# A feed-forward layer's third K tile: 64 channels padded with zeros to 128 rows

## The chip, the cores and the metric

The kernel runs on one core of a Trainium2 chip, as a single launch. The metric is the device time of the execution in microseconds (us), from the first to the last instruction; lower is better. All arithmetic is float32.

## What is computed

Two blocks follow each other. The first is a recurrence over 768 tokens, for 4 batches and 8 heads with 40 channels each; the second is a feed-forward layer on its 3072 output rows of 320 channels:

```
state = zeros(B, H, D, D)                       # B, H, S, D = 4, 8, 768, 40
for t in range(S):
    y[t]  = r[t] @ state
    Sa    = state @ a[t]
    state = state * w[t] - outer(Sa, b[t]) + outer(v[t], k[t])
x = y as (B*S, H*D)                             # 3072 x 320
h = x @ w_in                                    # 320 x 2048
out = (h - tanh(h)) @ w_out                     # 2048 x 320
```

## The kernel before

The recurrence goes in 24 chunks of 32 tokens, all batches and heads at once. `prep(c)` does what needs no state: transposes of the inputs (`p_nat`), products over tokens (`p_prod`), and the inverse of a triangular matrix, built in four doublings. Each doubling is a chain that passes from engine to engine: four transposes on TensorE (`p_flip`, line 246), a copy on ScalarE (`t`, line 247), four products (`p_g`), a masked multiplication on VectorE (`g`, line 280), four products (`p_z`), a subtraction on VectorE (`z`, line 285). `chain(c)` does what needs the state (`p_u`, `p_s`, `p_st`, `p_y`) and ends in `turn`, which transposes 128 tokens of the output by `p_x` and copies them into a half of `x_t` (in the profile `xT`), 128 rows of channels by 3 K tiles by 256 tokens. Its 320 channels are K tiles of 128, 128 and 64 (`KT`), so in the third tile rows 0 to 63 are written and read, by line 384.

After every second chunk the layer for 256 tokens is put on a list (`todo`), and `tick()` issues one piece of it at a time among the chains of the following chunks, so that TensorE has work while the chains wait. A piece is a pair of `w_in` blocks of 128 columns: into one PSUM bank `p_h` go, for each of the two blocks, three products over the K tiles (`mm` of line 85, with `w1` as the loaded weights and `x_t` streamed, 256 columns). The float32 product is two matmuls on the chip, each with a weight load of its own, so a pair of blocks is 12 matmuls. Then come ScalarE (tanh, and two squares, lines 397 to 399), GpSimd (403, 404) and VectorE (402, 405, 406, 408, 409), which leave h - tanh(h) in `gt`. Eight such pieces are followed by two products with `w2` (`p_o`, 16 blocks of 320 columns each, twice 32 matmuls), a copy (416) and a store. `p_h` and `p_o` share three PSUM banks (pool `psf`). The layer of the last 256 tokens has no chunk beside it and stands alone at the end; it will be called the last layer.

Once, at the start, the weights are loaded (`weights`), and constants are set on GpSimd. The scheduler of the language fixes each engine's order at build time; every engine then works in that order, and waits where its inputs are not there.

Each run of the two matmuls of a third K tile will be called a **visit**: there are 16 in a layer, 192 in the 12 layers, of which 176 stand among the chunks and 16 in the last layer.

Of the kernel before, what the change touches and what calls it, by code (L numbers as in the profile page):

```python
"""RWKV-7 state recurrence followed by a tanh-shrink feed-forward layer, on one core.

The recurrence runs over chunks of 32 tokens, all batches and heads at a time.  Inside a
chunk, with P the running product of the decays, it is a unit lower triangular system

    (I + N) U = -(A V + Â S0),   A[t,s] = â_t.k̂_s,  N[t,s] = â_t.b̂_s  (s < t)
    â_t = P[t-1] a_t,  k̂_s = k_s / P[s],  b̂_s = b_s / P[s]

whose inverse is built exactly, by doubling the inverted diagonal blocks from 1 to 32.
Then  Y = P[t-1] (R S0 + tril(R V^T) K̂ + tril(R U^T) B̂)  and  # L10
      S = P[31] (S0 + V^T K̂ + U^T B̂).
A tile of 128 partitions holds the 32 tokens of each of the four batches; the matrices
over tokens are block diagonal.  Heads go in pairs of 2 x 64 partitions (40 used) where
channels are on the partitions; states are kept per pair as block diagonal matrices.

All that holds for decays whose products over a chunk, and their quotients, fit float32.
The kernel looks at them, and at whether all outputs are finite; if need be it ends with
the recurrence token by token and the layer on its result.
"""
# [11 lines left out]
F32 = mybir.dt.float32  # L31
# [7 lines left out]
L = 32      # tokens in a chunk  # L39
DP = 64     # partitions that a head's channels take  # L40
P = 128
PR_MIN, PR_MAX = 1e-18, 1e12    # the products of a chunk's decays that the chunks' form is for

# h - tanh(h) = h s (C0 + s (C1 + C2 s + C3 s^2)), s = h^2 < SMALL^2, to 3e-9 of itself
SMALL = 0.25
C0, C1, C2, C3 = 0.33333333232863477, -0.13333281848327064, 0.05392688810132763, -0.02079906881679924
# C1 + C2 s + C3 s^2 = GAM - (SQ s + SQB)^2
SQ = math.sqrt(-C3)
# [5 lines left out]
def rwkv_shrink(ctx: ExitStack, tc: tile.TileContext, r, k, v, w, a, b, tok, dec, chan, w_in, w_out, out):  # L54
# [40 lines left out]
    # before[s, t] = 1 where s < t in one batch  # L95
# [4 lines left out]
    # pair_t[s, t] = -1 where s and t = s + 1 are a block of two  # L100
# [5 lines left out]
    # join[h][t, s] = 1 where t is in the second and s in the first half of one block of 2 h  # L106
    join = {}
# [9 lines left out]
    # own[p, b] = 1 where partition p is a token of batch b  # L117
# [4 lines left out]
    # half[p, e] = 1 where partition p is a channel of the pair's head e  # L122
# [4 lines left out]
    # what the scan of the decays adds: 1 before each batch's first token  # L127
# [5 lines left out]
    # of each chunk: the greatest and the least product of decays; 0, or NaN if an output isn't finite  # L133
# [6 lines left out]
    # the state, transposed: [(e, channel of k), batch, pair, e', channel of v], zero but for e = e'  # L140
# [7 lines left out]
    w1 = fixed("w1", [P, len(KT), DFF])  # L148
    w2 = fixed("w2", [P, NF, DM])
    WP = max(256, DM)  # L150

    def weight(dst, src, n):
        """A piece of a weight, [rows, n], into SBUF as float32."""
        rows = dst.shape[0]
        if src.dtype == F32:
            nc.sync.dma_start(out=dst, in_=src)
            return
        # float64 bits: sign 1, exponent 11, fraction 52, low word first (and values in float32's range).
        raw = ff.tile([P, WP, 2], I32, name="raw", tag="raw", bufs=1)[:rows, :n]
        nc.sync.dma_start(out=raw, in_=src.bitcast(I32).rearrange("p (n two) -> p n two", two=2))  # L160
        lo, hi = raw[:, :, 0], raw[:, :, 1]
        t_ = ff.tile([P, WP], I32, name="wt", tag="wt", bufs=1)[:rows, :n]
        f_ = ff.tile([P, WP], I32, name="wf", tag="wf", bufs=1)[:rows, :n]
        V.tensor_scalar(f_, hi, 0x07FFFFFF, 3, Alu.bitwise_and, Alu.logical_shift_left)
        V.tensor_scalar(t_, hi, -0x40000000, None, Alu.bitwise_and)
        V.tensor_tensor(f_, f_, t_, Alu.bitwise_or)
        V.tensor_scalar(t_, lo, 29, None, Alu.logical_shift_right)
        V.tensor_tensor(f_, f_, t_, Alu.bitwise_or)
        # to nearest: the first bit that is left out, added to the last one kept
        V.tensor_scalar(t_, lo, 3, 31, Alu.logical_shift_left, Alu.logical_shift_right)  # L170
        V.tensor_tensor(f_, f_, t_, Alu.add)
        # 0 below float32's normal numbers: the high words, as float32, rise with the magnitude
        V.tensor_scalar(t_, hi, 0x7FFFFFFF, None, Alu.bitwise_and)
        V.scalar_tensor_tensor(dst, t_.bitcast(F32), LEAST, f_.bitcast(F32), Alu.is_ge, Alu.mult)  # L174
# [12 lines left out]
    def tick():  # L187
        """The next piece of the layer, among the recurrence's chains."""
        while todo and next(todo[0], todo) is todo:
            todo.pop(0)  # L190

# [1 line left out]
    def prep(c):  # L193
# [10 lines left out]
        # the decays' running products: pr[..., i] is that of i tokens  # L204
# [3 lines left out]
        # (held to where quotients of them are sound: if one of them was not there, seen tells)  # L208
# [10 lines left out]
        # the state's decay over the chunk, for both halves of a pair  # L219
# [3 lines left out]
        # tokens on the partitions  # L223
# [45 lines left out]
        # z = ((I + N)^-1)^T by blocks of 2, 4, .. 32  # L269
# [20 lines left out]
        # -(I + N)^-1 A V and -((I + N)^-1 Â)^T  # L290
# [14 lines left out]
    def chain(c, g, x_t):  # L305
# [13 lines left out]
        if c > 0:  # L319
            # the old state's part of the output  # L320
            s_ = sb.tile([P, B, HP, 2, D], F32, name="s_", tag="s_")
            for b in range(B):
                p_ = bank("p_s")
                for q in range(HP):
                    T.transpose(p_[:, q * P:(q + 1) * P], st[:, b, q].rearrange("p e d -> p (e d)"), ident)  # L325
                A.copy(s_[:, b], p_.rearrange("p (q e d) -> p q e d", q=HP, e=2)[:, :, :, :D])
# [48 lines left out]
    def turn(yf, x_t, i_):  # L375
        """128 tokens of the layer's input, with the channels on the partitions."""
        p_ = bank("p_x")
        o_ = i_ * P
        for i, (r0, n) in enumerate(KT):
            T.transpose(p_[:n, i * P:(i + 1) * P], yf[:, r0:r0 + n], ident)  # L380
        full = sum(n == P for _, n in KT)
        A.copy(x_t[:, :full, o_:o_ + P], p_[:, :full * P].rearrange("p (k t) -> p k t", t=P))
        for i in range(full, len(KT)):
            A.copy(x_t[:KT[i][1], i, o_:o_ + P], p_[:KT[i][1], i * P:(i + 1) * P])

# [1 line left out]
    def layer(x_t, rows):  # L387
        gt = ff.tile([P, NF, 2 * P], F32, name="gt", tag="gt", bufs=1)
        for f in range(0, NF, 2):
            p_ = psf.tile([P, 512], F32, name="p_h", tag="pf")  # L390
            for i in range(2):
                for k_, (_, n) in enumerate(KT):
                    mm(p_[:, i * 2 * P:(i + 1) * 2 * P], w1[:n, k_, (f + i) * P:(f + i + 1) * P], x_t[:n, k_, :],
                       k_ == 0, k_ == len(KT) - 1)
            tile_ = lambda n_, b_=2, dt=F32: ff.tile([P, 512], dt, name=n_, tag=n_, bufs=b_)
            t_, s_, q_ = tile_("th"), tile_("sq"), tile_("qu")
            A.activation(t_, p_, Act.Tanh)  # L397
            A.activation(s_, p_, Act.Square)
            A.activation(q_, s_, Act.Square, bias=sqb, scale=SQ)  # L399
            o_ = gt[:, f:f + 2, :].rearrange("p f t -> p (f t)")  # L400
            # h - tanh(h), as it stands and, where that would cancel, by its series
            V.tensor_tensor(o_, p_, t_, Alu.subtract)
            G.tensor_scalar(q_, q_, -1.0, GAM, Alu.mult, Alu.add)  # L403
            G.tensor_tensor(q_, q_, s_, Alu.mult)  # L404
            V.scalar_tensor_tensor(q_, q_, C0, s_, Alu.add, Alu.mult)  # L405
            V.tensor_tensor(q_, q_, p_, Alu.mult)
            m_ = tile_("mk", 1, U8)
            V.tensor_scalar(m_, s_, SMALL * SMALL, None, Alu.is_lt)
            V.copy_predicated(o_, m_, q_)
            yield  # L410
# [9 lines left out]
    def slowly(sl):  # L420
# [29 lines left out]
        with tc.For_i(0, B * S, 2 * P) as r0:  # L450
            x_t = ff.tile([P, len(KT), 2 * P], F32, name="xT", tag="xT", bufs=2)
# [9 lines left out]
    for c in range(NCH):  # L461
        if c % 2 == 0:
            x_t = ff.tile([P, len(KT), 2 * P], F32, name="xT", tag="xT", bufs=2)
# [11 lines left out]
    # The quotients of products hold while these stay well inside float32.  Where they don't, or  # L475
    # something has overflowed, all is done anew, token by token.
# [52 lines left out]
```

## Time and profile before

| | |
|---|---|
| runs | 1999.52, 2021.6 and 2028.64 us; median 2021.6 us |
| span of the profiled execution | 2022.6 us |
| TensorE busy with matmuls | 1836.2 us (91%), 11978 matmuls |
| TensorE loading weights | 1474.7 us (73%) |
| VectorE, ScalarE, GpSimd busy | 1133.3, 478.0 and 401.6 us (56, 24 and 20%) |
| mean granted clock of TensorE | 0.879 |

The page gives no time of the profiled execution other than its span, which lies 1.0 us above the median of the three runs; these are 29 us apart. In the rows, PE is TensorE's matmuls, PEld its weight loads, DVE VectorE, ACT ScalarE and POOL GpSimd. A row of the timeline has the start, the length, the engine, the line, the operation, the tile written and the tiles read, rows of weights by columns, and the streamed size; "x8" is eight such instructions in a row, and a bracket tells how long the engine had been idle and what ended that. A matmul's length holds its way through the array, so matmuls that follow each other overlap; what one costs is the distance between starts. The granted clock is 1.00 or 0.50 in each stretch; a number between is a mean.

### The profile page before, as it was taken

How to read it: one execution, taken by the hardware profiler on the slowest of the kernel's cores; microseconds unless marked ns; L12 is line 12 of the kernel's file. 1: busy time of each engine (PE TensorE's matmuls, PEld its weight loads, DVE VectorE, ACT ScalarE, POOL GpSimd, SP SyncE). 2: the span in 40 equal slices, each digit the busy share in tenths (PEclk: the TensorE clock that was granted, in tenths of full speed). 3: DMA queues.
4: the chain of work that ended last, by engine and by line, in shares of the span. 5: the costliest groups of instructions: out<-in, count | busy, mean ns of one | idle time of the engine just before them, and what ended most of it. 6: DMA issues, size and time to landing. Idle time of an engine off the chain costs nothing.

```text
span 2022.6 us, 28394 instructions
## 1 busy us (share of the span) xinstructions
PE 1836.2 (91%) x11978; PEld 1474.7 (73%) x11978; DVE 1133.3 (56%) x1887; ACT 478.0 (24%) x909; POOL 401.6 (20%) x400
## 2 busy tenths in 40 slices
PE   4878897889999999899899899899899899989998
PEld 4767676777777877777777777777777777777865
DVE  6577768667465375474375375366365457347333
ACT  1011221113132132231132132132122123123121
POOL 4011130103122032031032032032022122122012
PEclk9977879798897899998898998988978979889867
DMA  3111011110101001001001010010010000100000
GB/s 104 52 36 54 13 42 45 61 60 15 38 5 35 30 13 39 30 9 39 30 10 36 7 36 31 12 35 27 16 36 14 29 30 1 36 27 1 7 1 8
DMA packets 18916, 58.17 MB, mean 29 GB/s; under 512 B 1888, under 2 KB 8032, under 8 KB 15712
## 3 DMA queue, kind: packets, MB, share of 16 engines
q1 hardware_dynamic: 18784, 56.30, 8.4%
q8 instruction: 96, 1.57, 0.3%
q14 instruction: 36, 0.29, 0.0%
HBM read 52.36 MB, written 3.93 MB: 28 GB/s over the span
## 4 chain that ended last, share of the span: by engine, by line
PE 79%; DVE 12%; POOL 4%; issue 2%; ACT 2%; DMA 1%; SPq 0%; ACTq 0%; DVEq 0%; POOLq 0%
PE p_h L85 16%; PE p_o L85 11%; PE p_g L85 10%; PE p_z L85 9%; PE p_y L85 8%; PE p_flip L246 5%; PE p_st L85 4%; DVE rp L212 4%; PE p_u L85 3%; PE p_nat L229 3%; PE p_av L85 3%; PE p_prod L85 3%; PE p_s L325 2%; DVE g L280 2%; POOL z L257 2%
## 5 line engine op out<-in xcount | busy, mean ns | idle before, releaser
L85 PE MATMUL p_h<-xT,w 128*128 128x256 f32 (+1 forms) x1152 | 395.4, 461 | 2.9 <-DVE w L174 2.4
L85 PEld LDWEIGHTS p_h<-xT,w 128*128 128x128 f32 (+1 forms) x1152 | 206.1, 213 | 131.3 <-issue 116.1
L85 PE MATMUL p_o<-w,gt 128*128 128x320 f32 x768 | 278.3, 491 | 0.2 <-DVE w L174 0.2
L85 PEld LDWEIGHTS p_g<-t,m 128*128 128x128 f32 x1536 | 217.5, 212 | 80.6 <-ACT t L247 70.6
L85 PE MATMUL p_g<-t,m 128*128 128x128 f32 x1536 | 238.4, 304 | 35.4 <-ACT t L247 35.4
L85 PE MATMUL p_z<-z,g 128*128 128x128 f32 x1536 | 228.6, 296 | 45.3 <-DVE g L280 45.3
L85 PEld LDWEIGHTS p_z<-z,g 128*128 128x128 f32 x1536 | 206.6, 205 | 84.9 <-DVE g L280 77.1
L280 DVE TENSOR_TENSOR g<-p_g,join 128x512 f32<-128x512 f32 x192 | 132.1, 688 | 185.1 <-PE p_g L85 184.6
L247 ACT COPY t<-p_flip 128x512 f32<-128x512 f32 x192 | 112.5, 586 | 472.9 <-PE p_flip L246 469.8
L285 DVE TENSOR_TENSOR z<-z,p_z 128x512 f32<-128x512 f32 x192 | 131.3, 684 | 136.3 <-PE p_z L85 135.4
L329 POOL TENSOR_TENSOR vb<-v_n,own 128x1280 f32<-128x1280 f32 x23 | 53.8, 2340 | 665.1 <-PE p_st L85 665.1
L85 PEld LDWEIGHTS p_o<-w,gt 128*128 128x128 f32 x768 | 148.2, 214 | 49.6 <-issue 19.9
L246 PE MATMUL p_flip<-ident,z 128*128 128x128 f32 x768 | 132.0, 294 | 40.0 <-POOL z L257 40.0
L403 POOL TENSOR_SCALAR qu<-qu 128x512 f32<-128x512 f32 x96 | 63.3, 659 | 509.6 <-ACT qu L399 509.3
L246 PEld LDWEIGHTS p_flip<-ident,z 128*128 128x128 f32 x768 | 100.1, 156 | 42.7 <-POOL z L257 42.5
L404 POOL TENSOR_TENSOR qu<-qu,sq 128x512 f32<-128x512 f32 x96 | 126.6, 1318 | 7.9
L212 DVE RECIPROCAL rp<-pr 128x512 f32<-128x512 f32 x24 | 80.4, 3352 | 74.4 <-PE p_nat L229 74.4
L405 DVE SCALAR_TENSOR_TENSOR qu<-qu,sq 128x512 f32<-128x512 f32 x96 | 66.3, 690 | 92.4 <-POOL qu L404 92.4
L85 PE MATMUL p_prod<-x_t 40*128 40x128 f32 x1152 | 112.1, 289 | 1.7 <-DVE st L343 1.7
L397 ACT ACTIVATE th<-p_h 128x512 f32<-128x512 f32 x96 | 57.3, 597 | 229.9 <-PE p_h L85 229.5
L85 PEld LDWEIGHTS p_prod<-x_t 40*128 40x128 f32 x1152 | 102.7, 191 | 10.7 <-issue 6.2
L214 POOL TENSOR_TENSOR x_t<-x_t,rp 128x512 f32<-128x512 f32 x24 | 31.0, 1293 | 369.5 <-DVE rp L212 369.5
(267 smaller groups left out, 2461.2 us busy)
## 6 DMA issues: line engine op xcount, KB each, us to landing
x_t<-in_chan SPq DMA_DIRECT2D x24, 1280.0 KB
w_t<-in_dec SPq DMA_DIRECT2D x24, 264.0 KB
raw<-in_w_out SPq DMA_DIRECT2D x16, 320.0 KB
raw<-in_w_in SPq DMA_DIRECT2D x16, 256.0 KB
v_n<-in_tok SPq DMA_DIRECT2D x24, 160.0 KB
raw<-in_w_in SPq DMA_DIRECT2D x8, 128.0 KB
out<-o__2684 SPq DMA_DIRECT2D x1, 160.0 KB
out<-o__2746 SPq DMA_DIRECT2D x1, 160.0 KB
```

The lines of the kernel that those rows point to most:

```text
L85: T.matmul(o, l_, r_, start=first, stop=last, skip_group_check=True)
L212: V.reciprocal(rp, pr_[:, :, 1:])
L229: T.transpose(p_[:, q * P:(q + 1) * P], x[:, q, :], ident)
L246: T.transpose(p_[:, q * P:(q + 1) * P], src[:, q, :], ident)
L247: A.copy(dst.rearrange("p q t -> p (q t)"), p_)
L280: V.tensor_tensor(gg, p_.rearrange("p (q t) -> p q t", q=HP), heads4(join[h_]), Alu.mult)
L285: V.tensor_tensor(z2.rearrange("p q t -> p (q t)"), z.rearrange("p q t -> p (q t)"), p2, Alu.subtract)
L329: G.tensor_tensor(vb, g["v"].rearrange("p h d -> p (h d)").unsqueeze(1).to_broadcast([P, B, DM]), own.unsqueeze(2).to_broadcast([P, B, DM] ...
L397: A.activation(t_, p_, Act.Tanh)
L403: G.tensor_scalar(q_, q_, -1.0, GAM, Alu.mult, Alu.add)
L404: G.tensor_tensor(q_, q_, s_, Alu.mult)
L405: V.scalar_tensor_tensor(q_, q_, C0, s_, Alu.add, Alu.mult)
```

## The change

The rows 64 to 127 of the third K tile are set to zero once, in `w1` and in two fixed buffers that take the place of the pool's two `xT` buffers, and the layer's products take all 128 rows. What is copied into `x_t` and loaded into `w1` stays as it was, 64 rows.

```
     w1 = fixed("w1", [P, len(KT), DFF])
+    x_bufs = [fixed(f"xT{i}", [P, len(KT), 2 * P]) for i in range(2)]
+    for k_, (_, n) in enumerate(KT):
+        if n < P:
+            G.memset(w1[n:, k_, :], 0.0)
+            for x_ in x_bufs:
+                G.memset(x_[n:, k_, :], 0.0)
...
                 for k_, (_, n) in enumerate(KT):
-                    mm(p_[:, i * 2 * P:(i + 1) * 2 * P], w1[:n, k_, (f + i) * P:(f + i + 1) * P], x_t[:n, k_, :],
+                    mm(p_[:, i * 2 * P:(i + 1) * 2 * P], w1[:, k_, (f + i) * P:(f + i + 1) * P], x_t[:, k_, :],
                        k_ == 0, k_ == len(KT) - 1)
...
         if c % 2 == 0:
-            x_t = ff.tile([P, len(KT), 2 * P], F32, name="xT", tag="xT", bufs=2)
+            x_t = x_bufs[c // 2 % 2]
```

On TensorE, VectorE, ScalarE and the DMA queue the instructions and their order stay the same. This is TensorE's order in the middle of a layer, in the chunk that the prediction takes its rows from, of the kernel before; there "x4" counts products, each of which is two matmuls:

```order
L246 MATMUL p_flip<-ident,z 128x128 x4
L85 MATMUL p_h<-xT,w_131 128x256 x3
L85 MATMUL p_g<-t,m 128x128 x4
L85 MATMUL p_h<-xT,w_131 128x256 x4
L85 MATMUL p_z<-z,g 128x128 x4
L246 MATMUL p_flip<-ident,z 128x128 x4
L85 MATMUL p_h<-xT,w_131 128x256 x2
L85 MATMUL p_g<-t,m 128x128 x4
L85 MATMUL p_h<-xT,w_131 128x256 x4
L85 MATMUL p_z<-z,g 128x128 x4
```

And of the change, at the same place, five of these rows:

```order
L253 MATMUL p_flip<-ident,z 128x128 x4
L85 MATMUL p_h<-xT_133,w_131 128x256 x2
L85 MATMUL p_g<-t,m 128x128 x4
L85 MATMUL p_h<-xT_133,w_131 128x256 x4
L85 MATMUL p_z<-z,g 128x128 x4
```

Nothing has moved; the name of the buffer and the line numbers after the inserted lines differ (line 246 is now 253). On GpSimd three instructions are added at the end of the constants, where `vb` is the first work for the recurrence. Before:

```order
L145 MEMSET u_nat_127 128x512
L145 MEMSET u_nat_128 128x512
L329 TENSOR_TENSOR vb<-v_n,own 128x1280
L221 TENSOR_TENSOR pc<-pr,half 128x32
L214 TENSOR_TENSOR x_t<-x_t,rp 128x512
```

And now:

```order
L145 MEMSET u_nat_127 128x512
L145 MEMSET u_nat_128 128x512
L153 MEMSET w_131 64x2048
L155 MEMSET xT_132 64x256
L155 MEMSET xT_133 64x256
L228 TENSOR_TENSOR pc<-pr,half 128x32
L336 TENSOR_TENSOR vb<-v_n,own 128x1280
L221 TENSOR_TENSOR x_t<-x_t,rp 128x512
```

The three settings to zero stand ahead of the first chunk's `pc` and `vb`, and these two have changed places; behind that GpSimd's order is as it was. (Here `x_t` is `prep`'s own tile of inputs, not the layer's.)

More of the change, by code (lines that the diff above doesn't have):

```diff
@@ L450, in slowly @@
         with tc.For_i(0, B * S, 2 * P) as r0:
-            x_t = ff.tile([P, len(KT), 2 * P], F32, name="xT", tag="xT", bufs=2)
+            x_t = x_bufs[0]
             for i in range(2):
@@ L462, in rwkv_shrink @@
         if c % 2 == 0:
-            x_t = ff.tile([P, len(KT), 2 * P], F32, name="xT", tag="xT", bufs=2)
+            x_t = x_bufs[c // 2 % 2]
         chain(c, g, x_t)
```

## The prediction

> **What bounds the kernel now.** I read the page first, then the groups with shapes kept apart, then the timeline at one place in the middle of a layer and at the end, and last the granted clock in single stretches.
>
> ```profile
> span 2022.6 us, 28394 instructions
> PE 1836.2 (91%) x11978; PEld 1474.7 (73%) x11978; DVE 1133.3 (56%) x1887; ACT 478.0 (24%) x909; POOL 401.6 (20%) x400
> PEclk9977879798897899998898998988978979889867
> PE 79%; DVE 12%; POOL 4%; issue 2%; ACT 2%; DMA 1%; SPq 0%; ACTq 0%; DVEq 0%; POOLq 0%
> ```
>
> TensorE is the bound, though not alone: 79% of the chain that ended last is its work, and 12 + 4 + 2% are VectorE, GpSimd and ScalarE. Its clock is not always full (the row of tenths, mean 0.879), so the worth of saved matmul time depends on where it is saved. The layer's first product, by shape:
>
> ```profile
> L85 PE MATMUL p_h<-xT,w 128*128 128x256 f32 x768 | 261.5, 451 | 0.5 <-ACT xT L382 0.5
> L85 PE MATMUL p_h<-xT,w 64*128 64x256 f32 x384 | 153.0, 483 | 2.4 <-DVE w L174 2.4
> L85 PEld LDWEIGHTS p_h<-xT,w 64*128 64x128 f32 x384 | 63.9, 208 | 69.3 <-issue 65.4 <-DVE w L174 2.9 <-DVE wt L165 0.3
> ```
>
> The reader should stop at the second row: a matmul over 64 rows takes no less than one over 128 (mean 483 against 451 ns), and TensorE is occupied 153.0 / 384 = 0.40 us by each, against 261.5 / 768 = 0.34 us. Half the rows cost more, and the 384 loads of these stand idle for 69.3 us, 65.4 of it without a cause that the profile shows. The timeline of the weight loads, then of the matmuls at full clock, shows why:
>
> ```profile
> 494.00 0.29 PEld L85 LDWEIGHTS p_h<-xT,w 64*128 64x128 f32 x2 [0.33 <-issue]
> 494.63 0.30 PEld L85 LDWEIGHTS p_h<-xT,w 128*128 128x128 f32 x2 [0.33 <-issue]
> ...
> 504.29 1.78 PE L85 MATMUL p_o<-w,gt 128*128 128x320 f32 x6
> 507.93 1.24 PE L85 MATMUL p_o<-w,gt 128*128 128x320 f32 x4
> ```
>
> The weight loads stop for 0.33 us ahead of the 64-row pair and again behind it, and wait for no other engine ("issue"). Elsewhere a load runs under the matmul before it; at a change between 64-row and 128-row work it does not. The Trainium skill ("TensorEngine Tiling (Array Packing)", Key Properties) says that changing the tiling mode drains TensorE; the two 0.33 us agree with it.
>
> **What a visit costs.** From the two `p_o` rows a matmul of 320 columns costs (1.78 - 1.24) / 2 = 0.27 us, so one of 256 costs 0.216.
>
> ```profile
> 489.14 0.60 ACT L397 ACTIVATE th<-p_h 128x512 f32<-128x512 f32 x1 [3.48 <-PE p_h L85]
> 491.77 1.31 POOL L404 TENSOR_TENSOR qu<-qu,sq 128x512 f32<-128x512 f32 x1
> 493.05 2.28 PE L85 MATMUL p_h<-xT,w 128*128 128x256 f32 x8
> 494.44 0.68 DVE L280 TENSOR_TENSOR g<-p_g,join 128x512 f32<-128x512 f32 x1
> 495.18 1.16 PE L85 MATMUL p_z<-z,g 128*128 128x128 f32 x8
> 500.45 0.60 ACT L397 ACTIVATE th<-p_h 128x512 f32<-128x512 f32 x1 [3.05 <-PE p_h L85]
> ```
>
> The eight `p_h` matmuls from 493.05 hold one visit. The next work, `p_z`, starts 2.13 us later; eight undisturbed ones would take 8 x 0.216 = 1.73. So a visit loses **0.39 to 0.40 us** at full clock, in its two changes of mode. The padded matmul I price as its neighbour over 128 rows, 0.216 us: nothing is added. 192 visits make 75 us, 69 in the 176 among the chunks.
>
> **Among the chunks half of it goes through.** In the rows above `g` ends at 495.12 and `p_z` starts at 495.18, just when TensorE is through with `p_h`: both are on time together. If TensorE comes earlier, it waits for `g`. VectorE does `g` behind lines 405 and 406, which wait for GpSimd's 404, which comes from the ScalarE work that began at 489.14. So the loop is: from 489.14 through ScalarE, GpSimd and VectorE to `p_z` at 495.18, 6.04 us that hold no visit's loss; then from there on TensorE to the end of the next pair but one at 500.45, 5.27 us with two visits in them (the order has one in each `p_h` group). The two together, 11.31 us, are two doublings with four visits; without the losses they take 6.04 + 5.27 - 2 x 0.39 = 10.53. Per visit 0.78 / 4 = 0.195 us arrive, half of 0.39; the rest becomes waiting of `p_z` for `g`, which is this now:
>
> ```profile
> PE p_z L85 <- DVE g L280: 45.3, 57, 1.6
> ```
>
> (us in total, times, longest). 176 x 0.195 = **34 us**. The ends are 0 (every chain as tight as VectorE's) and 69 (none); I take the loop's value.
>
> **The last layer.** It stands alone, and at half clock:
>
> ```profile
> 1945.83 50.52 PE L85 MATMUL p_h<-xT,w 128*128 128x256 f32 x96 [0.46 <-ACT xT L382]
> 1947.83 0.50 PEld L85 LDWEIGHTS p_h<-xT,w 64*128 64x128 f32 x2 [0.65 <-issue]
> 1950.98 0.50 PEld L85 LDWEIGHTS p_h<-xT,w 64*128 64x128 f32 x2 [0.65 <-issue]
> 1990.08 0.60 ACT L397 ACTIVATE th<-p_h 128x512 f32<-128x512 f32 x1 [4.47 <-PE p_h L85]
> 1996.39 0.60 ACT L397 ACTIVATE th<-p_h 128x512 f32<-128x512 f32 x1 [4.47 <-PE p_h L85]
> 1996.40 19.75 PE L85 MATMUL p_o<-w,gt 128*128 128x320 f32 x64
> 2002.32 0.73 DVE L409 COPY_PREDICATED gt<-mk,qu 128x512 f32<-128x512 uint8 x1
> 2016.19 0.43 ACT L416 COPY o__13235<-p_o 128x320 f32<-128x320 f32 x1 [8.19 <-PE p_o L85]
> ...
> 1945.83:1996.28 50.45, 50.45 (x96) 26.77 (x97) 20.11 (x34) 12.75 (x22) 15.35 (x14) 0.50 0.00 0
> 1997.58:2000.99 3.41, 3.41 (x8) 2.18 (x7) 1.58 (x3) 0.65 (x1) 2.24 (x2) 0.50 0.00 0
> 2000.99:2004.41 3.42, 3.42 (x14) 2.39 (x13) 2.07 (x5) 0.00 (x0) 0.00 (x0) 1.00 0.01 2
> ```
>
> The last three rows are stretches of time, with each engine's busy time and the granted clock third from the end. For 50 us TensorE is busy without a break and gets 0.50. Then `p_o` begins, all of it 128 rows without a change of mode, and from 2001 on, 4.6 us later, the clock is 1.00. My reading is that the clock follows how much of the array is fed. At half clock a 256-column matmul costs 2 x 0.216 = 0.43; a visit's period is 3.15 us (1947.83 to 1950.98), in which four matmuls feed all rows and two feed half of them: (4 + 2 x 1/2) x 0.43 / 3.15 = 0.68. In `p_o` it is 1. In a stretch inside the chunks the same can be seen:
>
> ```profile
> 468.41:471.82 3.41, 3.41 (x9) 1.93 (x9) 2.72 (x5) 0.22 (x1) 2.42 (x2) 0.50 0.00 0
> 471.82:475.23 3.41, 3.41 (x15) 3.23 (x16) 1.70 (x5) 0.59 (x1) 0.00 (x0) 0.50 0.00 0
> 475.23:478.65 3.42, 3.42 (x22) 2.81 (x21) 2.75 (x5) 1.29 (x3) 0.00 (x0) 1.00 0.28 78
> ```
>
> The first is nearly all one visit with its neighbours (9 matmuls; fed about 0.7) and the next stays at 0.50; the second has 15 full-height matmuls without a gap, and the third is at 1.00. So I expect the padded last layer, fed without gaps, to reach full clock some 5 us after its start. Then its matmuls cost 12 x 0.216 = 2.6 us for a pair of blocks and VectorE becomes the bound:
>
> ```profile
> 1958.55:1990.08 31.53, 14.75 (x25) 0.50 0.00 1
> ```
>
> This is VectorE alone from one pair's tanh to that of the fifth after it, 14.75 / 5 = 2.95 us for each; I take 3.0. The first pair is ready 12 x 0.43 = 5.2 us after 1945.83, at 1951.0; the eighth 7 x 3.0 = 21 us later, at 1972; its way through the engines is 6.7 us (1996.39 to 2003.05), to 1978.7; `p_o` then has four matmuls of its first half (1.1 us) and 32 of its second (8.6 us) to do, to 1988.4 where the rows have 2016.2. The gain is **27 us**. If the clock stays at half, 16 visits give back 3.15 - 6 x 0.43 = 0.57 us each, 9 us: the lower end. The upper end, full clock at once, adds 2 or 3.
>
> **The clock among the chunks.** A stretch such as 468.41 would be filled too, and the next one be at 1.00 already: up to 1.7 us of TensorE work saved, half of which arrives by the loop above, 0.85. I count one such stretch in each of 11 layers: **9 us**, between 0 and 11 x 1.7 = 19.
>
> **GpSimd at the start.**
>
> ```profile
> 6.33 1.80 POOL L142 MEMSET st<- 128x2048 f32 x1
> 9.60 2.54 POOL L329 TENSOR_TENSOR vb<-v_n,own 128x1280 f32<-128x1280 f32 x1
> 14.82 0.24 POOL L221 TENSOR_TENSOR pc<-pr,half 128x32 f32<-128x32 f32 x1 [2.68 <-DVE pr L210]
> 18.23 1.58 POOL L214 TENSOR_TENSOR x_t<-x_t,rp 128x512 f32<-128x512 f32 x1 [3.16 <-DVE rp L212]
> ```
>
> By the width of the 2048-column row the three settings take 1.80 + 2 x 0.23 = 2.3 us; they fall into the 2.68 and 3.16 us in which GpSimd waits for VectorE (`vb`'s 2.54 us, now behind `pc`, fit into the second). I count 0; without that cover it would be 2.3 us, once. No other wait is added: the two buffers of `xT` are two as before, and no DMA moves.
>
> **Sum.** Against the profiled 2022.6: 34 + 27 + 9 = 70 off. The median of the runs is 1.0 below that span, so 2021.6 - 70, rounded to **1952 us**.
>
> **The rivals.**
>
> - *The clock does not answer* (0.17). The last layer stays at 0.50 and no stretch is raised: 34 + 9 = 43 off, 1979 us. For it speaks that a whole 50 us of busy matmuls did not raise the clock, so that something other than what I count may hold it; against it that `p_o` raised it in 4.6 us. The Trainium skill ("TensorE: Matmul & The Clock Gate", Part 1, What's actually happening) has the gate open after about 3.4 us of sustained busy matmuls. By that rule busy time alone counts, which padding does not change; the trace disagrees with it where it has 0.50 over 50.45 busy us.
> - *All of it goes through* (0.12). If lines 405 and 406 move up with the earlier end of each pair, the wait of `p_z` does not grow: 69 + 27 + 19 = 115 off, 1907 us. The chain's 79% for TensorE speaks for it, the 0.06 us between `g` and `p_z` against it.
> - *The change does not remove the stall* (0.10). If the 0.33 us belonged to the third tile's place and not to its height, or if waiting chains took all of it, the time would be within some 15 us of now, about 2012. Against it: the 0.33 stands at both borders of the 64-row work, and the border of `p_o` to other 128-row work has none.
> - *More waiting lowers the clock* (0.03), on the other side. The half that becomes waiting makes holes in the layer's chunks, and holes cost clock. Each stretch of 3.41 us at 0.50 instead of 1.00 loses up to 1.7 us; with the last layer at half clock the gain is 43, so a loss of 2% needs (43 + 40) / 1.7 = 49 more such stretches, from 4.5 in each layer on; at 6 in each it is 11 x 6 x 1.7 - 43 = 69 more, 2091 us. Against it: padding feeds more rows in less time, so a stretch gets fuller.
>
> **How the numbers follow.** My forecast has 0.58; its own range is 1932 to 1972. The range of 8 in 10 goes down toward the case in which all goes through and up past that of the silent clock, 1912 to 1990. About 2% (40 us) is what a measurement of this kernel can tell from no change, as the three runs spread over 29 us; the border is 1981. Faster by more: 0.58 + 0.12 + 0.12 of the silent clock's 0.17 = 0.82. Within 2%: 0.05 + 0.10 = 0.15. Slower: 0.03.
>
> **What would show it.** In the profile after: no 64-row `p_h` group, 1152 of one shape, and loads of `p_h` without 0.33 us ahead of them; if those stay, the first step is wrong. `p_z` waiting for `g` longer in total than 45.3 us, by some tens: the half that does not arrive; if it doesn't grow, more goes through. The last layer's `p_h` about 27 us instead of 50, at a clock near 1 after some 5 us, with VectorE almost without idle; if it takes about 41, the clock did not answer. The forecast fails most easily in the clock, since its stretches fall differently in every execution.

## The result, and the profile after

The median of the changed kernel is 1912.55 us (four runs, 1904.34 to 1932.43), of the kernel before, run beside it, 2012.87 us (four runs, 1999.52 to 2028.64). The ratio is 0.9524, with a 95% interval of 0.9445 to 0.9603: **faster by 4.8%**, 100 us by the medians, where 70 were forecast. The time lies below the forecast's own range (1932 to 1972 us) and just inside the wider one (1912 to 1990). The direction held; the size was too small, and the sections below say which term was. A second batch of the same two kernels, described below, gave 84 us by the medians and a ratio of 0.9628, so a part of the 30 us that are missing may be the spread of the runs. (Medians are of all runs; the ratios and their intervals are of those within some 1.5% of their kernel's fastest run, so the two can differ.)

The page of the changed kernel, the same four rows that were shown of before:

```profile
span 1902.6 us, 28396 instructions
PE 1693.0 (89%) x11978; PEld 1430.7 (75%) x11978; DVE 1146.7 (60%) x1887; ACT 475.1 (25%) x909; POOL 403.4 (21%) x403
PEclk9878979899898999899999989989879899899989
PE 62%; DVE 21%; POOL 7%; ACT 5%; issue 3%; DMA 2%; SPq 0%; ACTq 0%; DVEq 0%; POOLq 0%
```

The span is 120 us shorter, the number of matmuls the same. TensorE is busy 143 us less, and its part of the chain falls from 79 to 62%, while VectorE's grows from 12 to 21%: a good part of what TensorE no longer does has become waiting for others. In the clock's row the last slices, before at 6 and 7 tenths, are at 8 and 9. The mean granted clock is 0.917 instead of 0.879 (0.894 to 0.912 in the other three runs).

The first product by shape, and its loads:

```profile
L85 PE MATMUL p_h<-xT,w 128*128 128x256 f32 x1152 | 302.2, 399 | 4.9 <-DVE qu L413 2.7 <-DVE w L181 1.6 <-ACT xT L389 0.5
L85 PEld LDWEIGHTS p_h<-xT,w 128*128 128x128 f32 x1152 | 214.1, 200 | 33.2 <-PE p_h L85 4.6 <-DVE w L181 2.1 <-issue 1.4
```

One shape is left, 1152 of it, with 302.2 us where the two shapes had 261.5 + 153.0 = 414.5: 112 us less. The loads' idle time put down to "issue" is 1.4 us; it was 65.4 at the 64-row loads and another 50.7 at the 128-row ones.

The timeline of two doublings in the middle of a layer, at the place that the prediction reckoned with (lines 404, 411 and 287 are 397, 404 and 280 of before):

```profile
455.90 0.60 ACT L404 ACTIVATE th<-p_h 128x512 f32<-128x512 f32 x1 [2.90 <-PE p_h L85]
458.53 1.32 POOL L411 TENSOR_TENSOR qu<-qu,sq 128x512 f32<-128x512 f32 x1
459.55 1.89 PE L85 MATMUL p_h<-xT,w 128*128 128x256 f32 x8
461.21 0.68 DVE L287 TENSOR_TENSOR g<-p_g,join 128x512 f32<-128x512 f32 x1
461.95 1.16 PE L85 MATMUL p_z<-z,g 128*128 128x128 f32 x8 [0.51 <-DVE g L287]
466.71 0.60 ACT L404 ACTIVATE th<-p_h 128x512 f32<-128x512 f32 x1 [2.54 <-PE p_h L85]
```

The eight `p_h` matmuls take 1.89 us instead of 2.28. `p_z` now waits 0.51 us for `g`, which comes 0.06 us ahead of it, as before: from the tanh at 455.90 to `p_z` it is 6.05 us, and was 6.04. What has become shorter is the other leg, to the next tanh but one: 4.76 us instead of 5.27.

The waits of the changed kernel (us in total, times, longest):

```profile
PE p_z L85 <- DVE g L287: 66.8, 108, 2.8
```

It was 45.3 us in 57 waits. The growth goes with the stalls, and not with the rows that are fed or with the clock: the runs of the next section have 64.7 to 66.8 us where the `p_h` products are free of stalls, whatever their rows, and 45.3 to 46.6 where they are not. (The runs that halve the changes of mode, or leave out or move other work of the layer, are not among these.) Two of them, over 87 rows without stalls and over 72 and 64 rows with them:

```profile
PE p_z L85 <- DVE g L287: 65.1, 101, 1.9
PE p_z L85 <- DVE g L280: 45.7, 57, 1.6
```

The last layer, first its rows in the timeline and then its stretches (length, busy time of TensorE, its loads, VectorE, ScalarE and GpSimd, the granted clock third from the end; the last row is VectorE alone):

```profile
1851.49 9.58 PE L85 MATMUL p_h<-xT,w 128*128 128x256 f32 x36 [0.46 <-ACT xT L389]
1871.64 2.83 PE L85 MATMUL p_h<-xT,w 128*128 128x256 f32 x12 [0.64 <-DVE qu L413]
1875.11 2.83 PE L85 MATMUL p_h<-xT,w 128*128 128x256 f32 x12 [0.64 <-DVE qu L413]
1878.58 17.57 PE L85 MATMUL p_o<-w,gt 128*128 128x320 f32 x64 [0.52 <-DVE qu L413]
...
1851.49:1856.50 5.01, 5.01 (x16) 4.15 (x17) 0.00 (x0) 0.68 (x3) 0.00 (x0) 0.69 0.00 0
1856.50:1878.00 21.50, 18.77 (x84) 14.75 (x82) 19.07 (x29) 12.11 (x22) 11.62 (x13) 1.00 0.00 1
...
1861.91:1875.75 13.84, 13.84 (x22) 1.00 0.00 0
```

It begins at half clock, as before, but only for some 3.1 us (a mean of 0.69 over the first 5.01 us is 0.50 over 3.1 of them and 1.00 over the rest), and then has 1.00 through the last of these rows. Its `p_h` takes from 1851.49 to `p_o` at 1878.58, 27.1 us instead of 50.6. TensorE now stops ahead of each pair (0.64 us), for a bank that line 413 on VectorE has to free, and VectorE is busy without a gap.

Three stretches of the chunks, each from one turn of tokens (`p_x`) to the next, first of before and then of after. The first two rows are a chunk with eight pairs of the layer beside it, the next two its neighbour, which has the `w2` products, and the last two are the first chunk, which has nothing of the layer:

```profile
1007.20:1091.80 84.60, 82.56 (x536) 64.55 (x537) 55.16 (x86) 26.84 (x49) 23.89 (x23) 0.90 0.08 26
953.40:1031.50 78.10, 73.95 (x535) 62.80 (x536) 56.43 (x86) 26.68 (x49) 24.09 (x23) 0.96 0.08 24
1091.80:1164.40 72.60, 64.30 (x473) 54.53 (x471) 29.89 (x43) 13.05 (x27) 8.46 (x7) 0.90 0.07 25
1031.50:1103.60 72.10, 63.78 (x472) 54.14 (x470) 29.88 (x44) 12.95 (x27) 8.46 (x7) 0.91 0.08 29
0.00:103.50 103.50, 66.53 (x340) 58.10 (x340) 62.37 (x120) 12.00 (x20) 24.84 (x54) 0.97 0.23 77
0.00:90.70 90.70, 55.28 (x341) 48.19 (x341) 62.34 (x120) 11.98 (x20) 26.88 (x57) 0.96 0.27 87
```

The chunk with the pairs is 6.5 us shorter, and its clock higher (0.96 for 0.90); its neighbour has not changed. The first chunk is 12.8 us shorter though nothing of the change is in it. That is chance, as other executions show below. So the 120 us of this profile are 13 in the first chunk, 26 from the last `p_x` to the end (78.1 us before, 52.5 after), and most of the other 81 in the chunks with the pairs: the twelve chunks with over 500 matmuls have a mean of 86.5 us before and 79.8 after, 12 x 6.6 = 79. The spans of the two profiles are 120 us apart and the medians 100, so these figures are somewhat too large; a table below has other executions beside them.

### The profile page after: what moved, and what is told of

It reads as the page before. It is cut to its first block, busy times and chain, and to the rows that moved or that the text cites. A ratio compares the mean times of both kernels' runs of the same rounds, so it can differ in the third digit from the quotient of the medians.

```text
span 1902.6 us, 28396 instructions
## 1 busy us (share of the span) xinstructions
PE 1693.0 (89%) x11978; PEld 1430.7 (75%) x11978; DVE 1146.7 (60%) x1887; ACT 475.1 (25%) x909; POOL 403.4 (21%) x403
## 4 chain that ended last, share of the span: by engine, by line
PE 62%; DVE 21%; POOL 7%; ACT 5%; issue 3%; DMA 2%; SPq 0%; ACTq 0%; DVEq 0%; POOLq 0%
PE p_o L85 10%; PE p_z L85 8%; PE p_y L85 8%; PE p_g L85 7%; PE p_h L85 5%; PE p_st L85 4%; DVE rp L219 4%; PE p_flip L253 4%; PE p_prod L85 3%; DVE g L287 3%; PE p_u L85 3%; PE p_av L85 3%; PE p_nat L236 3%; POOL qu L411 2%; PE p_s L332 2%
## 5 line engine op out<-in xcount | busy, mean ns | idle before, releaser
L85 PE MATMUL p_h<-xT,w 128*128 128x256 f32 x1152 | 302.2, 399 | 4.9 <-DVE qu L413 2.7
L85 PEld LDWEIGHTS p_z<-z,g 128*128 128x128 f32 x1536 | 195.2, 197 | 121.5 <-DVE g L287 119.9
L85 PE MATMUL p_z<-z,g 128*128 128x128 f32 x1536 | 223.4, 290 | 67.5 <-DVE g L287 66.8
L85 PEld LDWEIGHTS p_g<-t,m 128*128 128x128 f32 x1536 | 210.0, 207 | 76.6 <-ACT t L254 69.6
L85 PE MATMUL p_o<-w,gt 128*128 128x320 f32 x768 | 263.6, 470 | 0.7 <-DVE qu L413 0.5
L85 PE MATMUL p_g<-t,m 128*128 128x128 f32 x1536 | 231.8, 298 | 35.4 <-ACT t L254 35.4
L85 PEld LDWEIGHTS p_h<-xT,w 128*128 128x128 f32 x1152 | 214.1, 200 | 33.2 <-PE p_h L85 4.6
L85 PEld LDWEIGHTS p_o<-w,gt 128*128 128x128 f32 x768 | 142.5, 205 | 44.6 <-issue 11.4
```

The lines of the kernel that those rows point to most:

```text
L85: T.matmul(o, l_, r_, start=first, stop=last, skip_group_check=True)
```

## The experiments

Each batch had runs of the kernel before beside it; their medians were 2005.78 us (buffers alone, 65 rows, 72 rows, neighbours), 2010.34 us (the two without the series, 72 rows with a 64-row third tile, the mask on GpSimd) and 2007.01 us (the change again, 87 rows, the mask on ScalarE).

**The buffers and settings alone.** The change with products over 64 rows, as before:

```diff
-  w1[:, k_, (f + i) * P:(f + i + 1) * P], x_t[:, k_, :]
+  w1[:n, k_, (f + i) * P:(f + i + 1) * P], x_t[:n, k_, :]
```

> Undoes the main part: the rows are set to zero and the two fixed buffers are there, but the layer's third product takes 64 rows as before. Both theories: as before, within 1.5% (1985 to 2030 us), the last layer's first product 50.5 us at clock 0.50, 0.33 us ahead of and behind each 64-row pair. A rival that puts the gain on the buffers or on GpSimd's new order at the start would have about 1912.

Measured: 2013.57 us (10 runs), ratio 1.0056 (1.0002 to 1.0111). The fixed buffers and GpSimd's three settings bring no gain; all of the gain is in the rows that the products take.

**65 rows.** One row of zeros instead of 64:

```diff
-  w1[:, k_, (f + i) * P:(f + i + 1) * P], x_t[:, k_, :]
+  w1[:max(n, 65), k_, (f + i) * P:(f + i + 1) * P], x_t[:max(n, 65), k_, :]
```

> Pads the third tile to 65 rows in place of 128: just over the 64 at which the mode changes. Fill theory (stalls cost time by themselves, and the clock follows the rows fed): no 0.33 us stalls; the last layer is fed (4 + 2 x 0.51) / 6 = 0.84, more than the 0.68 that stayed at half clock, so its clock rises; a little more half clock among the chunks than with 128 rows; 1915 to 1945 us. Rival (the clock follows unbroken matmul time, rows don't matter): the same as with 128 rows, 1905 to 1930. If the last layer stays at 0.50 with its first product at 41 us, the limit lies above 0.84.

Measured: 1924.71 us (4 runs), ratio 0.9685 (0.9604 to 0.9766). Its group of the third tile:

```profile
L85 PE MATMUL p_h<-xT,w 65*128 65x256 f32 x384 | 122.7, 402 | 1.7 <-DVE w L181 1.6
```

A matmul over 65 rows occupies TensorE for 122.7 / 384 = 0.32 us, against 0.40 over 64, and from the last `p_x` of this kernel to its end it is 52.8 us, against 52.5 in the change. The step lies between 64 and 65 rows, as a change of tiling mode would have it. In the Trainium skill ("TensorEngine Tiling (Array Packing)", Key Properties) the drain comes with a switch of mode; the runs agree. One row more than before can feed the array hardly more, so what this kernel gained in clock (0.917 in its profile, as in that of the change) it gained from the stalls that are gone. The other 63 rows of zeros bring nothing that these runs can tell: the change has ratios of 0.9524 and 0.9628.

**72 rows in all three tiles.** The instructions, their order and the absence of a stall as in the change, but the first two tiles without 56 of their channels each, so that only 72 / 128 = 0.56 of the array is fed:

```diff
-  w1[:, k_, (f + i) * P:(f + i + 1) * P], x_t[:, k_, :]
+  w1[:72, k_, (f + i) * P:(f + i + 1) * P], x_t[:72, k_, :]
```

> All three K tiles take rows 0 to 71 alone, so 56 channels of each of the first two tiles are left out of the layer. No change of mode, matmuls as many and as long as in the change, but each feeds 72 / 128 = 0.56 of the array. Fill theory: the last layer stays at clock 0.50, its first product 96 x 0.43 = 41 us; among the chunks more half clock than in the change; 1940 to 2000 us. Rival (unbroken matmul time counts): as the change, 1905 to 1930, the last layer's first product about 27 us.

Measured: 1995.08 us (10 runs), ratio 0.998 (0.993 to 1.003). Its last layer, the row and the stretch:

```profile
1939.15 41.33 PE L85 MATMUL p_h<-xT,w 72*128 72x256 f32 x96 [0.46 <-ACT xT L389]
1939.15:1980.40 41.25, 41.25 (x96) 32.27 (x96) 19.23 (x33) 12.74 (x22) 15.29 (x14) 0.50 0.00 0
```

41.25 us of matmuls without a break or a stall, all at 0.50. They take 96 x 0.43 us, the time that the prediction gave for a silent clock. Nothing but the rows is different from the change, whose clock was full within 5 us. So the clock answers to **the rows that are fed**, not to how long TensorE is busy. The rule of the Trainium skill ("TensorE: Matmul & The Clock Gate", Part 1, What's actually happening), that some 3.4 us of sustained busy time open the gate, does not hold in these 41.25 us. And the stalls that are gone are paid back in clock: the kernel is no faster than before.

**The 64-row products made neighbours.** No padding; the second block's K tiles in reverse, so that two visits become one of four matmuls, with half the changes of mode:

```diff
-  for k_, (_, n) in enumerate(KT):
+  for j, (k_, (_, n)) in enumerate(list(enumerate(KT))[::1 - 2 * i]):
```

(with the start and the end of the sum by `j`)

> No padding: the kernel before with the K tiles of the second block of a pair taken in the order third, second, first, so that the two 64-row products of a pair stand next to each other and one change into the mode and back serves both. Half the stalls are left (96 x 0.39 = 37 us of 75). Both theories: about half the change's gain, 1960 to 1990 us. Fill theory for the last layer: (8 + 4 x 0.5) x 0.43 / (12 x 0.43 + 0.57) = 0.75, at the limit's unknown place: first product 46 us if the clock stays, 27 to 32 if it rises.

Measured: 1978.49 us (4 runs) against 2005.78, 27 us less, and some quarter to a third of what padding brings. No interval is on record for it: its runs go from 1951.11 to 1992.52, those of the kernel before from 1980.04 to 2026.27. Its last layer, the first two rows of which are parts of the third:

```profile
1915.94:1919.40 3.46, 3.46 (x8) 2.34 (x8) 0.00 (x0) 0.11 (x1) 0.00 (x0) 0.50 0.00 0
1922.80:1926.20 3.40, 3.40 (x16) 2.19 (x14) 1.16 (x3) 1.83 (x4) 1.96 (x2) 1.00 0.00 0
1915.94:1931.36 15.42, 15.41 (x48) 10.29 (x48) 5.16 (x9) 5.53 (x10) 5.26 (x6) 0.78 0.00 0
1931.36:1945.00 13.64, 12.72 (x51) 8.26 (x50) 13.64 (x22) 7.27 (x13) 7.30 (x8) 1.00 0.00 1
```

Here the clock rises too, within 7 us (0.78 over 15.42 us is 0.50 over 6.8 of them). In the two profiles it takes 54.6 us from the last `p_x` to the end, where the kernel before takes 78.1, so most of this kernel's gain is in the last layer. By the prediction's measure this order feeds (8 + 4 x 1/2) x 0.43 / (12 x 0.43 + 0.58) = 0.75 of the array in the mean, in stretches that differ among each other.

**87 rows in all three tiles.** 41 channels of each of the first two left out. 87 / 128 = 0.68 of the array is fed, as much as the prediction's reckoning gave for the kernel before with its stalls, but without them:

```diff
-  w1[:, k_, (f + i) * P:(f + i + 1) * P], x_t[:, k_, :]
+  w1[:87, k_, (f + i) * P:(f + i + 1) * P], x_t[:87, k_, :]
```

> All three tiles take rows 0 to 86, which leaves out 41 channels of each of the first two tiles: no change of mode, and each matmul feeds 87 / 128 = 0.68 of the array, as much as the kernel before feeds in a visit's period, stalls included. So the stalls are gone and the feeding is held. Fill theory: the last layer stays at clock 0.50 with its first product at 41 us; 43 to 45 us off the kernel before (the stalls alone), 1955 to 1975, and some 50 us above the change, which is the clock's part. Rival (stalls are what the clock answers to, rows hardly count): the change's time, 1905 to 1930, last layer's first product about 27 us.

Measured: 1960.66 us (5 runs, 1942.15 to 2003.97), ratio 0.9764 (0.9621 to 0.9908). Its last layer:

```profile
1935.41 41.33 PE L85 MATMUL p_h<-xT,w 87*128 87x256 f32 x96 [0.46 <-ACT xT L389]
1935.50:1976.50 41.00, 41.00 (x96) 32.09 (x96) 19.05 (x32) 12.67 (x22) 15.29 (x14) 0.50 0.00 0
```

0.50 for 41 us again. This kernel parts the gain in two: the stalls alone are 2007.01 - 1960.66 = 46 us, the clock is the rest. All five runs lie above all eight of the change, if by 0.3 us at the nearest (the highest of those is 1941.82), so that the second part is likely there; its size is 1960.66 - 1922.59 = 38 us against the change in the same batch and 48 against the 1912.55 of the first. By the ratios of the batch it is (0.9764 - 0.9628) x 2007 = 27 us, with intervals of some 1.5% on either ratio.

**72 rows with a 64-row third tile.** The 72-row kernel with its stalls, on the base of before:

```diff
-  w1[:n, k_, (f + i) * P:(f + i + 1) * P], x_t[:n, k_, :]
+  w1[:min(n, 72), k_, (f + i) * P:(f + i + 1) * P], x_t[:min(n, 72), k_, :]
```

> As the run in which all three tiles take rows 0 to 71, but the third takes its 64 rows and so keeps its two changes of mode; 56 channels of the first two tiles are left out. Both feed so little (0.56 and 0.44 of the array) that the last layer is at half clock in both; the difference between them is what the stalls cost by themselves. By the prediction's terms 34 among the chunks + 9 in the last layer = 43 us more than the run with 72 rows in all: 2020 to 2050 us, and above the kernel before. Rival (the stalls are worth most of the 95 us that the change brings, the clock little): 70 us or more above it, over 2060.

Measured: 2039.86 us (4 runs), ratio 1.0107 (1.0027 to 1.0186), 29.5 us above its kernel before by the medians, where the 72-row kernel is 10.7 below its own: the stalls alone are 40 us by the medians, 25 by the ratios (1.0107 - 0.998 of 2007), against 43 of the prediction. Its last layer:

```profile
1960.50 50.52 PE L85 MATMUL p_h<-xT,w 72*128 72x256 f32 x96 [0.46 <-ACT xT L382]
```

50.52 us, the length of before to the hundredth, where without stalls it is 41.33: 9.2 us for the 16 visits at half clock, and 9 were reckoned.

**Without the series' arithmetic, 64 and 128 rows.** To test the loop, the lines through which the prediction had it go are left out, `p_h` as before and as changed:

```diff
-            G.tensor_scalar(q_, q_, -1.0, GAM, Alu.mult, Alu.add)
-            G.tensor_tensor(q_, q_, s_, Alu.mult)
-            V.scalar_tensor_tensor(q_, q_, C0, s_, Alu.add, Alu.mult)
-            V.tensor_tensor(q_, q_, p_, Alu.mult)
```

> The kernel before without the series: GpSimd's lines 403 and 404 and VectorE's 405 and 406 are left out, so small h is not corrected. VectorE's g then stands behind nothing that waits for GpSimd. It serves as the base for the next run. By the loop of the prediction (half of a visit's loss is hidden by that wait) the kernel before gains little by this itself, p_z's wait for g falls from 45 to under 40 us, and the time is 1970 to 2010 us. Rival (the loop through GpSimd is not what holds p_z): the wait stays at about 45 us.

> The change without the series, to be held against the run before it. Loop theory: with g early, all of a visit's 0.39 us arrives, 69 us among the chunks in place of 34, and p_z's wait for g does not grow; with the clock's part as in the change and the last layer's 27 to 30 us, the difference to the run with 64 rows is 120 to 145 us. Rival (the hidden half is hidden by something else, or there is no hidden half): the same difference as the change itself made, 93 to 100 us.

Measured: 1942.31 us (4 runs, ratio 0.963, 0.9574 to 0.9687) with 64 rows, faster than expected, and 1840.55 us (4 runs, ratio 0.914, 0.9081 to 0.9199) with 128. The waits of `p_z`, first with 64 and then with 128 rows:

```profile
PE p_z L85 <- DVE g L280: 32.3, 43, 1.6
PE p_z L85 <- DVE g L287: 33.6, 43, 1.6
```

The wait no longer grows with the padding, as the loop would have it. But padding brings 101.8 us here, hardly more than the 100 with the series (84 in the repeat), where the loop let expect 20 to 45 more. So the loop's number did not come; whether something else than the cover of `g` keeps saved time from arriving, or the spread of the runs hides the difference, these runs do not tell.

**The mask on GpSimd.** In the change, line 408 of before (415 now) moves from VectorE to GpSimd:

```diff
-            V.tensor_scalar(m_, s_, SMALL * SMALL, None, Alu.is_lt)
+            G.tensor_scalar(m_, s_, SMALL * SMALL, None, Alu.is_lt)
```

> A version to beat the change: the change with the mask of line 408 on GpSimd in place of VectorE, which takes 0.52 us per pair off VectorE, 2.95 us per pair in the last layer. If VectorE's throughput holds the last layer and the middle chunks, 1890 to 1905 us; if GpSimd's place in the loop (its work is ahead of line 405) or its slower instruction holds them, 1910 to 1940.

Measured: 1995.42 us (4 runs), ratio 0.9855 (0.9767 to 0.9943), 73 to 83 us slower than the change; both expectations missed. The wait of `p_z`, and GpSimd's mask, first as a group and then twice in the timeline:

```profile
PE p_z L85 <- DVE g L287: 117.1, 114, 2.7
L415 POOL TENSOR_SCALAR mk<-sq 128x512 uint8<-128x512 f32 x96 | 147.3, 1535 | 363.5 <-ACT sq L405 214.5 <-DVE gt L416 142.0 <-DVE wf L173 3.4
475.68 1.49 POOL L415 TENSOR_SCALAR mk<-sq 128x512 uint8<-128x512 f32 x1 [2.86 <-DVE gt L416]
482.07 1.49 POOL L415 TENSOR_SCALAR mk<-sq 128x512 uint8<-128x512 f32 x1 [2.85 <-DVE gt L416]
```

`p_z` waits for `g` 117.1 us instead of 66.8. But the edit did more than add an operation to GpSimd. The mask stands ahead of lines 410 and 411 in GpSimd's order, takes 1.5 us there (0.65 in the mean on VectorE), and its tile `mk` has one buffer, so it has to wait for VectorE's copy (line 416) of the pair before: 142.0 us in all. That closes a ring of its own: copy, next mask, 410, 411, 412, 413, `g`, copy, at 482.07 - 475.68 = 6.39 us for a pair. So the slowdown is explained by what the edit added, and does not tell whether GpSimd's work holds the change's own loop, which was the prediction's reading.

**The mask on ScalarE.** In the change, VectorE's mask is replaced by a second activation on ScalarE, whose result is positive where `s` is below the threshold:

```diff
-            m_ = tile_("mk", 1, U8)
-            V.tensor_scalar(m_, s_, SMALL * SMALL, None, Alu.is_lt)
-            V.copy_predicated(o_, m_, q_)
+            A.activation(t_, s_, Act.Relu, bias=thr, scale=-1.0)
+            V.copy_predicated(o_, t_.bitcast(I32), q_)
```

> A version to beat the change: the change with the mask of line 408 made by ScalarE (the positive part of the limit minus s, written over the tanh's tile and read as integers), 0.52 us per pair off VectorE and nothing more on GpSimd, whose work stands in the loop. If VectorE's queue holds the middle chunks and the last layer, 1885 to 1905 us; if the latency from the pair's end through GpSimd holds them, 1905 to 1925, no gain.

Measured: 1917.02 us (4 runs), ratio 0.9566 (0.9424 to 0.9708), against 1922.59 for the change in the same batch: no difference that can be measured. An instruction less on VectorE, with one more on ScalarE in its place, does not shorten the loop enough to be seen.

**The change again.**

> The change once more, beside the other runs of this batch, to have it and the kernel before on one chip: 1905 to 1930 us, 0.95 to 0.96 of before. The 13 us by which its first profile was shorter in the first chunk, where there is no visit, come by where the clock's stretches happen to lie, if they are gone in this profile; if they are there again, they belong to the change (GpSimd's new order at the start).

Measured: 1922.59 us (4 runs, 1907.54 to 1941.82), ratio 0.9628 (0.9486 to 0.9769). Its first chunk:

```profile
0.00:109.20 109.20, 74.67 (x341) 64.63 (x341) 61.21 (x120) 12.00 (x20) 26.90 (x57) 0.98 0.22 73
```

109.2 us, where the first profile of the change had 90.7 and before 103.5, with TensorE busy 74.67 us on the same 341 matmuls for which it took 55.28 there. (The records of the clock begin within these stretches and not at their start, so the clock column cannot be used for them.) The run with the 64-row products as neighbours, which starts as the kernel before does, has its first `p_x` at 91.1 us. The 13 us of the first chunk are therefore not the change's.

## Why the prediction was right, and where it was too small

**The stall and its price: right.** No 64-row group is left, the loads' "issue" went from 65.4 to 1.4 us, and eight matmuls with a visit went from 2.28 to 1.89 us, 0.39 less. That it is the border of 64 rows, and not the place of the third tile, is shown by the 65 rows. The rival in which the stall stays has fallen.

**Half of it arrives among the chunks, 34 us: the size holds within wide intervals, the reason in part.** The 87 rows give 46 us for the stalls alone, 9 to 10 of them in the last layer, so 36 among the chunks (with an interval of some 30 us on either side); the pair of 72-row kernels gives 25 to 40 with the last layer (some 20 us on either side of the 25). All 69 lie outside both intervals; nothing at all lies outside the first, if barely. In the timeline two doublings take 10.81 us, where 11.31 were measured before and 10.53 worked out: at this one place 0.50 of 4 x 0.39 = 1.56 us arrive, a third and not a half. The leg that holds `g` did not move by more than 0.01 us, and the wait of `p_z` grew by 21.5 us, "some tens", in this and every other run without stalls that keeps the layer's work as it was: the covered part becomes waiting, as predicted. Without the series the wait did not grow, yet hardly more of the gain came. So that the leg through GpSimd sets how much arrives is argued from the timeline and not shown; the mask on GpSimd can't decide it, since it closed a ring of its own.

**The last layer, 27 us: right.** From the last `p_x` to the end it is 78.1 - 52.5 = 25.6 us less. `p_h` took 27.1 us where some 27 were predicted; the clock was full within 5 us; VectorE became the bound. One factor was off: the pairs follow each other by 1875.11 - 1871.64 = 3.47 us, not 3.0, which makes some 3 us over seven pairs; its cause is in the last section. The rival of the silent clock is what the 72 and the 87 rows do, and its 41 us and its 9 us came out there to a few tenths. The 87-row run bears on the prediction's reading most directly: the same 0.68 and no stall, and the clock stays. With the 65 rows, which feed (4 + 2 x 65/128) / 6 = 0.84 and rise, the limit at half clock lies above 0.68 and not above 0.84; the neighbours rise too, at 0.75 in the mean, but in uneven stretches. It is rows and stalls together that count, the rows fed per time: 65 rows without stalls rise where 64 with them stay, and 87 without stalls stay.

**The clock among the chunks, 9 us: the term that was mis-sized.** It measured 12 to 32 us: from the 87 rows to the change 27 (by the ratios), 38 (medians of the batch) or 48 (first median of the change), less the last layer's 68.2 - 52.5 = 15.7, by the lengths from the last `p_x` to the end in the two profiles. The step that failed is "I count one such stretch in each of 11 layers"; its upper end of 19 us lies inside what was measured. The twelve chunks with over 500 matmuls, by windows like those above, in the mean:

| kernel | span of the profile, us | length, us | granted clock | time at half clock, us |
|---|---|---|---|---|
| before | 2022.6 | 86.5 | 0.876 | 22.0 |
| the buffers and settings alone | 1991.0 | 84.5 | 0.896 | 17.9 |
| the change | 1902.6 | 79.8 | 0.927 | 12.0 |
| the change again | 1940.0 | 80.5 | 0.917 | 13.7 |
| 65 rows | 1914.5 | 79.7 | 0.931 | 11.4 |
| 87 rows | 2002.3 | 84.8 | 0.858 | 24.5 |

(The last column is the length times twice what the clock lacks of 1.) The first two rows have the same work on TensorE and differ by 4.1 us, which is what one execution of a kernel can differ from another here. The time at half clock falls by 17.9 - 13.7 = 4.2 to 22.0 - 12.0 = 10.0 us in a chunk, which is 1.2 to 2.9 stretches of 3.41 us and not one. With the prediction's own price of 0.85 us each that makes 12 x 1.2 x 0.85 = 12 to 12 x 2.9 x 0.85 = 30 us. That fits the 12 to 32 measured, so one was most likely too small a count; the price by itself was not tested. The count came from one place in the trace, the stretch at 468.41, where the time at half clock of all these chunks would have been the thing to sort by its causes. The 87 rows, without stalls, have no less time at half clock than before, and the 65 rows, with hardly more rows than before and without stalls, have as little as the change: the stalls' holes count by what they take from the rows fed per time.

**All goes through** (1907 us) lies nearest to the 1912.55 measured, but its mechanism did not happen: it had the wait of `p_z` not grow and 69 us of stalls arrive, and instead the wait grew and some 36 arrived; the rest is the last layer, the clock and the spread of the runs. **More waiting lowers the clock** did not come: `p_z` waits more and the clock is higher, since the stretches are fuller.

**GpSimd at the start, nothing: right.** The settings alone are at 1.0056, within the bound. The rows at the start of the changed kernel:

```profile
9.66 1.80 POOL L153 MEMSET w<- 64x2048 f32 x1
11.41 0.56 POOL L155 MEMSET xT<- 64x256 f32 x2
16.55 1.58 POOL L221 TENSOR_TENSOR x_t<-x_t,rp 128x512 f32<-128x512 f32 x1 [0.88 <-DVE rp L219]
```

They take 2.3 us, and GpSimd still waits 0.88 us for VectorE ahead of its next work, where it waited 3.16: the cover was used and was enough.

## What to carry to other kernels

A last K tile of 64 rows between tiles of 128 can cost more than the rows it saves: look in the trace for weight loads that stand idle ahead of and behind it with no releaser, and pad it, since the padded rows cost nothing in the matmul's time (here one row more than 64 was enough). Then ask what the padding does to the clock, stage by stage: count the fed rows in each stretch that was at half clock, and not only in the one that stands alone. And of a stall that is removed in a loop through several engines, expect that only a part arrives; the engine to look at next may be one that is busy a fifth of the time. When an operation is moved to another engine, see first how many buffers its result has: with one, the move can add a wait that costs more than the operation.

## What the runs showed of the hardware

The prediction had argued from 50 us of before that the clock follows the fed rows. How much hangs on it was not expected: from 72 rows to 128 the same instructions in the same order, with no stall in either, differ by 1995.08 - 1912.55 = 83 us (73 against the second median of the change), nearly the whole gain of either batch (100 and 84).

A second thing was not expected. In the last layer of the changed kernel VectorE's copy of line 416 (409 of before) takes twice its time, 1.44 us where the prediction's row of before had 0.73. VectorE and GpSimd in the timeline there, and the last copy, which has no work of GpSimd beside it:

```profile
1868.55 1.44 DVE L416 COPY_PREDICATED gt<-mk,qu 128x512 f32<-128x512 uint8 x1
...
1868.13 1.27 POOL L411 TENSOR_TENSOR qu<-qu,sq 128x512 f32<-128x512 f32 x1
...
1885.39 0.73 DVE L416 COPY_PREDICATED gt<-mk,qu 128x512 f32<-128x512 uint8 x1
```

GpSimd's product runs until 1869.40, and the copy ends 0.59 us behind it. In each pair of that stretch but the last the two overlap like this, and the copy is long in each; that more than accounts for the 3.47 us of a pair instead of 3.0. The whole trace of the changed kernel bears it out: of its 96 copies ten take over 1 us, and each of the ten overlaps a two-input product of GpSimd; the other 86 take 0.71 to 0.76 us, and none of them does (two run beside GpSimd's one-input line 410 and are not longer). So the copy is held up beside such a product; by what, no run shows.
